# Pair features by products with neighbour steps spread over rows by DMA, a bf16 copy on ScalarE, and two shared PSUM banks

## The chip, the cores and the metric

The kernel runs on one core of a Trainium2 chip. The metric is the device time of one execution in microseconds. Three runs of the kernel before gave 366.8, 369.47 and 370.51 us; the median is 369.47 us. A separate, profiled execution is where all durations below come from.

In the profile, PE is TensorE (matrix products), PEld its weight loads, DVE is VectorE, ACT is ScalarE, POOL is GpSimd and SP is SyncE. POOL and SP here mostly issue DMAs. L505 means line 505 of the kernel before.

## The reference

An attention block with 32 inducing points is followed by a feed-forward layer. `x` has 4 batches of 12480 tokens with 128 channels; `inducing` has 32 rows.

```
def mab(q, kv):
    s = scale * (q @ kv.transpose(0, 2, 1))        # scale = 1 / sqrt(128)
    s = s - s.max(-1, keepdims=True)
    a = np.exp(s)
    a /= a.sum(-1, keepdims=True) + 1e-09
    return a @ kv
h = mab(I, x)              # 32 rows per batch, from all tokens
y = mab(x, h)              # every token, a mix of the 32 rows of h
u = y @ w_in               # 128 -> 2048
out = (u * np.clip(u + 3.0, 0.0, 6.0) / 6.0) @ w_out
```

## The kernel before

**The algebra.** A token's `y` is a weighted mean of the 32 rows `h_m`, so the output can be written as a linear part in the 32 normalised weights minus a part that is quadratic in them: for each pair of rows `(m, n)` a product of the two weights times a coefficient vector made from the square of `(h_m - h_n) @ w_in`. The 496 pairs are laid out as four blocks of 128 rows (the features). A feature is `exp(scale * (h_m + h_n) . x)`, the product of two unnormalised weights. So each token costs four features of 128 rows, one 128x128 matmul for each, one linear matmul, and one multiplication by the inverse of the squared sum of the weights.

**Tiling.** A batch has six groups of 2048 tokens and a last one of 192. A group has four chunks of 512 tokens (the last group one chunk of 192), so there are 25 chunks per batch, 100 in all. In a chunk the tokens are four slices of 128.

**Three kinds of work.**

- *Stage a* of a batch (`a_T`, `a_s1`, `a_agg`), per group: 16 transposes of a bf16 copy of x on TensorE into a PSUM tile `pt`, each half copied by DVE into `xT` (L214, L215); 16 score matmuls into `s1` (L222), one exp on ACT (L228), then 16 aggregation matmuls that accumulate `exp @ x` in the bank `hnd` (L236) and a DVE sum of the weights (L247). x comes in from memory through POOL's DMA queue (L116). For batch 0 the bf16 copy is made half by DVE and half by ACT (L204, L205); for the other batches x is read a second time by a DMA that converts it (L120).
- *Stage c* of a batch (`c_sum` to `c_tail`): the 32 rows of h, their transpose `HT`, differences `dH` and sums `W` (L327 to L341); G, L and BD, the linear part (L349 to L393); and `c_sq`, 16 times: a matmul of `w_in` with `dH` into `dpm` (L400), its square, on ACT (L411) or in batch 0 every fourth time on DVE (L408, L409), and two units later four matmuls that accumulate the coefficients in the bank `cp` (L420). `c_tail` copies them to `Cq` (L433).
- *Stage b*, per chunk: `b_base` three times, a matmul of `W[:, k]` with the chunk's `xT` into a bank `bp` (L505) and an exp on ACT (L512), which gives T0, D1 and D2; three products on DVE, T1 = T0 D1, T2 = T0 D2, T3 = T2 D1 (L519, L528, L529); the linear matmul (L537) and 16 feature matmuls (L553) into a bank `op`; and the eviction, which multiplies by `r_all` on DVE (L569) and after each group's last chunk is followed by an output DMA on SP's queue (L576). Per group there are also `b_e`, four matmuls of 32 columns into four strips of one bank and an exp, `b_f` and `b_r`, which make the weights' sums and inverses.

**What sets the order.** The order on each engine is the order in which the program is written (a manual schedule); each engine works through its own list in order and waits where an operand isn't ready. The loop runs over chunks `t`. In iteration t the matmuls of chunk t are issued, the features of chunk t + 2 are begun (`LEAD = 2`), and the products of chunk t + 1 are finished. The per-group work is put into iterations shortly before the group's first chunk (`ahead`). Between these pieces the function `bg` puts units of background work, four times an iteration: the stages a and c of the next batch, as a list of 66 units spread evenly over the 25 iterations of this batch. Stage a and c of batch 0 run before the loop and in its first four iterations (the prelude); the last batch has no background work.

**PSUM.** There are eight banks: three rotating ones for `bp`, `ep`, `sp`, `rp` and other small results, two for `op`, one for `pt` and `dpm`, one for `s1` and `cp`, and one that `hnd`, `gp`, `lp` and `lt` use one after another. In batch 0 `pt` and `dpm` take turns over the `op` banks too.

Of the kernel before, what the change touches and what calls it, by code (L numbers as in the profile page):

```python
# [9 lines left out]
FP32 = mybir.dt.float32  # L10
# [15 lines left out]
SL = 4  # L26
LEAD = 2


def shifted(t, off, k_step, i_step):  # L30

    a = t[:, 0, 0:1]
    return bass.AP(
        tensor=a.tensor, offset=a.offset + off, ap=[a.ap[0], [k_step, 2], [i_step, 4], [1, 32]]
    )


def shifted1(t, off, i_step):

    a = t[:, 0, 0:1]  # L40
    return bass.AP(tensor=a.tensor, offset=a.offset + off, ap=[a.ap[0], [i_step, 4], [1, 32]])
# [3 lines left out]
def kernel(  # L45
# [38 lines left out]
    with ExitStack() as es:  # L84
# [3 lines left out]
        xin = es.enter_context(tc.tile_pool(name="xin", bufs=4))  # L88
# [3 lines left out]
        dp = es.enter_context(tc.tile_pool(name="dp", bufs=3))  # L92
# [3 lines left out]
        sqp = es.enter_context(tc.tile_pool(name="sqp", bufs=3))  # L96
# [15 lines left out]
        def load_x(b, g):  # L112
# [5 lines left out]
            if b > 0:  # L118
                tb = xbin.tile([P, TG, C], BF16, name="xb")
                nc.gpsimd.dma_start(tb[:p, :n, :], src)  # L120
                xbs[(b, g)] = tb

        for g in range(4):
            load_x(0, g)
# [23 lines left out]
        sel = sel[:, :, :].rearrange("k q m -> k (q m)")  # L148

# [32 lines left out]
        def side_bank(b, shape, dtype, name):  # L182

            if b == 0:
                turn[0] += 1
                if turn[0] % 3:
                    return psO.tile(shape, dtype, name=name, tag="op")
# [11 lines left out]
        def a_cast(g):  # L199
            t0, p, n = groups[g]  # L200
            h = n // 2
            xb = xbin.tile([P, TG, C], BF16, name="xb")
            xbs[(0, g)] = xb
            nc.vector.tensor_copy(xb[:p, :h, :], xs[(0, g)][:p, :h, :].bitcast(FP32))  # L204
            nc.scalar.copy(xb[:p, h:n, :], xs[(0, g)][:p, h:n, :].bitcast(FP32))  # L205
# [11 lines left out]
        def a_s1(b, g):  # L217
            t0, p, n = groups[g]
            st = S[b]
            s1 = psS.tile([P, 512], FP32, name="s1", tag="s1")  # L220
# [10 lines left out]
        def a_agg(b, g, h, a1):  # L231
# [18 lines left out]
            else:  # L250
                ahead = 4 if b == 0 else 2
                if g + ahead < NGR:
                    load_x(b, g + ahead)
                if b == 0 and g + ahead == NGR - 1:
                    load_weights()

        def a_units(b):
# [3 lines left out]
            for g in range(NGR):  # L261
# [6 lines left out]
                us.append(lambda g=g: a_T(b, g, 0))  # L268
                if late:
                    us.append(late.pop(0))  # L270
                us.append(lambda g=g: a_T(b, g, 1))
# [8 lines left out]
        def a_first():  # L280

            a_cast(0)
# [571 lines left out]
```

## Time and profile before

| | |
|---|---|
| runs | 366.8, 369.47, 370.51 us (median 369.47) |
| the profiled execution: time | 371.26 us |
| its span | 369.4 us |
| mean granted TensorE clock | 0.978 |
| busy: PE, DVE, ACT, POOL | 330.9, 284.4, 238.7, 28.7 us |
| DMA | 63.52 MB in 12516 packets |

The span is cut by stage: x loads and stage a of batch 0 until about 35 us, the prelude until about 59 us, three batch periods of about 83.5 us that carry the next batch's stages a and c, a last batch of about 50 us, and some 9 us at the end in which the last store lands.

How to read the rows: a row of the timeline has the start and the length in us, the engine, the line, what is written from what is read, and the count; in brackets stands how long the engine was idle before it, and what released it. Matmuls are pipelined, so the length of one is more than what it holds the engine for; the distance from one start to the next tells that. A row of the chain of waits has start, length and the work that the end of the run depended on. A row of a group by line has the shapes, the count, then busy us and mean ns, then the idle time before and its releasers.

### The profile page before, as it was taken

The page shows a single profiled execution, that of the slowest core. Times are in us where ns is not written, and L with a number is a line of the kernel's source. Part 1 is how long each engine was busy: PE and PEld are TensorE (multiplying, and loading weights), DVE is VectorE, ACT ScalarE, POOL GpSimd, SP SyncE. Part 2 cuts the span into 40 slices and gives each one's busy share as a digit, 9 for nine tenths or more (in the row PEclk, how much of TensorE's full clock was granted, in tenths as well). Part 3 has the DMA queues.
Part 4 walks back from the last instruction along what each step waited for, and adds up shares of the span by engine and source line. Part 5 has one row for each costly group of instructions (what it writes and reads, how often), then busy time and mean ns, then how long its engine had stood idle before and what let it go on. Part 6 is the DMA issues. An engine that isn't in the chain of part 4 may idle for free.

```text
span 369.4 us, 9414 instructions
## 1 busy us (share of the span) xinstructions
PE 330.9 (90%) x3926; PEld 246.8 (67%) x3926; DVE 284.4 (77%) x688; ACT 238.7 (65%) x442; POOL 28.7 (8%) x57
## 2 busy tenths in 40 slices
PE   1848977999989998999989998999989999999980
PEld 1737555887767675878757775888757766767760
DVE  3746577989897767989897767988887768999990
ACT  2432465666677875566667875566667887888840
POOL 3022001111100001111100001120000000000000
PEclk9988899999999999999999999999999999999995
DMA  7699802999982204998982204997022203222241
GB/s 271 232 350 241 287 0 31 307 277 216 300 262 114 115 3 142 291 295 207 313 262 118 112 4 135 280 291 237 16 101 115 113 4 126 115 114 115 115 184 67
DMA packets 12516, 63.52 MB, mean 172 GB/s; under 512 B 1280, under 2 KB 3504, under 8 KB 6192
## 3 DMA queue, kind: packets, MB, share of 16 engines
q0 software_dynamic: 8704, 37.24, 38.0%
q1 hardware_dynamic: 3760, 25.58, 17.0%
q8 instruction: 33, 0.54, 0.6%
q14 instruction: 19, 0.16, 0.1%
HBM read 46.84 MB, written 25.56 MB: 196 GB/s over the span
## 4 chain that ended last, share of the span: by engine, by line
PE 74%; DVE 14%; DMA 4%; ACT 4%; issue 2%; POOL 0%; POOLq 0%; DVEq 0%
PE op L553 22%; PE bp L505 14%; PE hnd L236 6%; PE pt L214 6%; PE op L537 5%; DMA xr<-in_x_dram 4%; PE dpm L400 4%; PE cp L420 3%; DVE os L569 3%; PE s L222 3%; PE ep L455 2%; PE rp L490 2%; PE gp L349 2%; PE sp L469 2%; DVE T L529 2%
## 5 line engine op out<-in xcount | busy, mean ns | idle before, releaser
L512 ACT ACTIVATE x<-bp 128x512 bf16<-128x512 f32 x300 | 170.8, 586 | 68.8 <-PE bp L505 60.8
L553 PE MATMUL op<-Cq,T 128*128 128x128 bf16 (+1 forms) x1200 | 130.6, 219 | 0.4
L505 PE MATMUL bp<-xT,W 128*128 128x512 bf16 x300 | 112.0, 374 | 0.0
L553 PEld LDWEIGHTS <-T 128*128 128x128 bf16 (+1 forms) x1200 | 84.2, 98 | 13.0 <-DVE T L529 0.8
L553 PE MATMUL op<-Cq,x 128*128 128x128 bf16 (+1 forms) x400 | 89.8, 224 | 0.0
L569 DVE TENSOR_TENSOR os<-op,r_all 128x512 f32<-128x512 f32 (+1 forms) x100 | 68.5, 685 | 21.0 <-PE op L553 20.3
L553 PEld LDWEIGHTS <-x 128*128 128x128 bf16 (+1 forms) x400 | 38.7, 97 | 27.9 <-issue 21.4
L519 DVE TENSOR_TENSOR T<-x,x 128x512 bf16<-128x512 bf16 (+1 forms) x100 | 41.4, 414 | 14.1 <-ACT x L512 13.4
L537 PE MATMUL op<-BD,nf 128*128 128x512 f32 (+1 forms) x100 | 51.9, 519 | 0.0
L529 DVE TENSOR_TENSOR T<-T,x 128x512 bf16<-128x512 bf16 (+1 forms) x100 | 41.8, 418 | 3.4
L215 DVE COPY xT<-pt 128x1024 bf16<-128x1024 bf16 (+1 forms) x56 | 34.4, 616 | 11.8 <-PE pt L214 11.7
L236 PE MATMUL hnd<-xr,a 128*32 128x128 f32 (+1 forms) x400 | 40.6, 244 | 1.5 <-ACT a L228 1.4
L528 DVE TENSOR_TENSOR T<-x,x 128x512 bf16<-128x512 bf16 (+1 forms) x100 | 40.9, 409 | 0.0
L214 PE MATMUL pt<-ident_b,xb 128*128 128x128 bf16 (+1 forms) x400 | 33.6, 230 | 7.5 <-DVE xT L215 4.1
L411 ACT ACTIVATE sq<-dpm 128x512 bf16<-128x512 f32 x60 | 35.4, 595 | 6.7 <-PE dpm L400 6.6
L214 PEld LDWEIGHTS <-xb 128*128 128x128 bf16 (+1 forms) x400 | 27.0, 104 | 13.6 <-issue 6.5
L236 PEld LDWEIGHTS hnd<-xr,a 128*32 128x32 f32 (+1 forms) x400 | 29.2, 113 | 7.5 <-ACT a L228 2.2
L420 PEld LDWEIGHTS <-sq 128*128 128x128 bf16 x256 | 19.1, 97 | 18.6 <-issue 5.7
L505 PEld LDWEIGHTS <-W 128*128 128x128 bf16 x300 | 29.3, 98 | 0.9
L420 PE MATMUL cp<-w6n,sq 128*128 128x128 bf16 x256 | 24.6, 219 | 2.2 <-DVE sq L409 2.2
L400 PE MATMUL dpm<-dH,w_in_b 128*128 128x512 bf16 x64 | 24.1, 379 | 2.0 <-ACT sq L411 1.7
L120 POOL DMA_DIRECT2D xb<-in_x_dram x21 | 11.1, 530 | 190.4 <-PE pt L214 125.9
(94 smaller groups left out, 304.9 us busy)
## 6 DMA issues: line engine op xcount, KB each, us to landing
xr<-in_x_dram POOLq DMA_DIRECT2D x24, 1024.0 KB, 7.8
out_dram<-os SPq DMA_DIRECT2D x24, 1024.0 KB, 4.3
xb<-in_x_dram POOLq DMA_DIRECT2D x18, 512.0 KB, 6.5
w_in_r<-in_moe_w_in_dram POOLq DMA_DIRECT2D x1, 1024.0 KB, 6.7
w_out_r<-in_moe_w_out_dram POOLq DMA_DIRECT2D x1, 1024.0 KB, 9.6
xr<-in_x_dram POOLq DMA_DIRECT2D x4, 96.0 KB, 7.1
out_dram<-os SPq DMA_DIRECT2D x4, 96.0 KB, 2.3
xb<-in_x_dram POOLq DMA_DIRECT2D x3, 48.0 KB, 2.6
```

The lines of the kernel that those rows point to most:

```text
L214: nc.tensor.transpose(pt[:, (i - lo) * p : (i - lo + 1) * p], xb[:p, i, :], ident_b[:p, :p])
L236: nc.tensor.matmul(st["hnd"][:M, :C], lhsT=a1[:p, i * M : (i + 1) * M], rhs=xs[(b, g)][:p, i, :], start=(g == 0 and i == 0), stop=(g == NG ...
L400: nc.tensor.matmul(dpm[:, :], lhsT=w_in_b[:, jb * P : (jb + 1) * P], rhs=st["dH"][:, :, :, :, :].rearrange("p q k i m -> p (q k i m)"),)
L420: nc.tensor.matmul(st["cp"][:, k * C : (k + 1) * C], lhsT=sq[:, k * P : (k + 1) * P], rhs=w6n[:, jc, :], start=(jc == 0 and k == 0), stop= ...
L505: nc.tensor.matmul(bp[:, :w], lhsT=st["W"][:, k].rearrange("p i m -> p (i m)"), rhs=st["xT"][:, c0 : c0 + w],)
L512: nc.scalar.activation(t[:, :w], bp[:, :w], ACT.Exp, scale=scale)
L519: nc.vector.tensor_mul(T1[:, :w], st[("x", c, 0)][:, :w], st[("x", c, 1)][:, :w])
L528: nc.vector.tensor_mul(T2[:, :w], T0[:, :w], D2[:, :w])
L529: nc.vector.tensor_mul(T3[:, :w], T2[:, :w], D1[:, :w])
L537: nc.tensor.matmul(op[:p, :], lhsT=st[("nf", g)][:, j * p : (j + 1) * p], rhs=st["BD"][:, :], start=True, stop=False, skip_group_check=True,)
L553: nc.tensor.matmul(op[:p, s * C : (s + 1) * C], lhsT=T[k][:, s * p : (s + 1) * p], rhs=st["Cq"][:, k, :], start=False, stop=(s == SL - 1 a ...
L569: nc.vector.tensor_mul(ot[:p, j * SL : (j + 1) * SL, :], op[:p, :].rearrange("p (s c) -> p s c", c=C), r_all[:p, b, c, :].unsqueeze(2).to_ ...
```

## The change

Seven edits belong together.

1. **Features.** The pairs are laid out anew: T0 holds the pairs of rows at distance 2, 6, 10, 14, T3 those at distance 4, 8, 12, 16, with the four distances next to each other for one m. Both are made by a base matmul and an exp, so two per chunk in place of three. T1 and T2 (odd distances) are T0 times a factor that depends on m alone: `exp(scale * (h_{m+1} - h_m) . x)` and `exp(scale * (h_{m-1} - h_m) . x)`. So DVE makes two products per chunk in place of three.
2. **Pack and spread.** The two factors have 32 rows. `b_pack` makes them for a whole group at once: four matmuls of 32 columns, one for each chunk, into four strips of one bank, then one exp on ACT; twice per group. `b_spread` copies for each chunk and factor the 32 rows to 128, each row four times, by a DMA on SP's queue (128 KB written), four chunks ahead; the product that reads it is issued three iterations later.
3. **bf16 copy.** x is read once. ACT converts it from the fp32 tile in two halves per group, each put behind a burst of transposes (`a_cast`). Batch 0 keeps its split between DVE and ACT. x loads are issued four groups ahead in all batches, over the batch's end too.
4. **Banks.** `pt`, `s1` and `dpm` share two banks. `cp` moves to the bank that `hnd`, `gp`, `lp` and `lt` use.
5. **Squares.** The coefficient matmuls follow their square by six units instead of two, with eight buffers for squares instead of three; G, L and BD come earlier in the list of units. The list has 69 units.
6. **Tail.** The pairs at distance 16 count half. They are now every fourth row of the last block, so a column of factors `half_of`, made at the start, takes the place of a constant for a range of rows.
7. **Prelude.** The loop begins one iteration earlier, at t = -5.

```diff
@@ a_cast, in place of the second read of x
+        def a_cast(b, g, parts):
+            t0, p, n = groups[g]
+            if (b, g) not in xbs:
+                xbs[(b, g)] = xbin.tile([P, TG, C], BF16, name="xb")
+            xb = xbs[(b, g)]
+            for eng, lo, hi in parts:
+                lo, hi = lo * n // 4, hi * n // 4
+                eng(xb[:p, lo:hi, :], xs[(b, g)][:p, lo:hi, :].bitcast(FP32))
@@ a_units
+                def first(g=g):
+                    a_T(b, g, 0)
+                    if g + 1 < NGR:
+                        a_cast(b, g + 1, ((nc.scalar.copy, 0, 2),))
+                def second(g=g):
+                    a_T(b, g, 1)
+                    if g + 1 < NGR:
+                        a_cast(b, g + 1, ((nc.scalar.copy, 2, 4),))
@@ pools
-        dp = es.enter_context(tc.tile_pool(name="dp", bufs=3))
+        dpk = es.enter_context(tc.tile_pool(name="dpk", bufs=2))
+        dp = es.enter_context(tc.tile_pool(name="dp", bufs=4))
-        sqp = es.enter_context(tc.tile_pool(name="sqp", bufs=3))
+        sqp = es.enter_context(tc.tile_pool(name="sqp", bufs=8))
-        psX = es.enter_context(tc.tile_pool(name="psX", bufs=1, space=PSUM))
-        psS = es.enter_context(tc.tile_pool(name="psS", bufs=1, space=PSUM))
+        psX = es.enter_context(tc.tile_pool(name="psX", bufs=2, space=PSUM))
@@ c_HT
+            W = coef.tile([P, 2, M, 4], BF16, name="W")
+            nc.vector.tensor_add(W[:, :], shifted(HT, 0, 0, 0), shifted(HT, 2, 2, 4))
+            Wd = coef.tile([P, 2, M], BF16, name="Wd")
+            nc.vector.tensor_sub(Wd[:, 0], HT[:, :, :].rearrange("p a m -> p (a m)")[:, 1 : M + 1], HT[:, 0])
+            nc.vector.tensor_sub(Wd[:, 1], HT[:, :, :].rearrange("p a m -> p (a m)")[:, M - 1 : 2 * M - 1], HT[:, 0])
@@ c_sq
-            jc = jb - 2
+            jc = jb - CLAG
-                st["cp"] = psS.tile([P, 512], FP32, name="cp", tag="s1")
+                st["cp"] = psH.tile([P, 512], FP32, name="cp", tag="hnd")
@@ c_units
+            us = [lambda: c_sum(b)] + gap + [lambda: c_den(b)] + gap + [lambda: c_HT(b)] + gap
+            us += sq[0:1] + [lambda: c_G(b, 0), lambda: c_G(b, 1)] + sq[1:3]
+            us += [lambda: c_L(b, 0), lambda: c_L(b, 1)] + sq[3:5] + [lambda: c_BD(b)]
+            us += sq[5:] + [lambda: c_tail(b)]
@@ new
+        def b_pack(b, g, k):
+            t0, p, n = groups[g]
+            st = S[b]
+            J = n // SL
+            w = SL * p
+            pp = psF.tile([P, 512], FP32, name="pp", tag="fb")
+            for j in range(J):
+                nc.tensor.matmul(
+                    pp[32 * j : 32 * j + 32, :w],
+                    lhsT=st["Wd"][:, k],
+                    rhs=st["xT"][:, t0 + j * w : t0 + (j + 1) * w],
+                    tile_position=(0, 32 * j),
+                )
+            t = dpk.tile([P, 512], BF16, name=f"dk{k}")
+            nc.scalar.activation(t[: 32 * J, :w], pp[: 32 * J, :w], ACT.Exp, scale=scale)
+            st[("dk", g, k)] = t
+        def b_spread(b, c):
+            g, j = chunks[c]
+            st = S[b]
+            w = SL * groups[g][1]
+            for k in range(2):
+                d = dp.tile([P, 512], BF16, name=f"d{k}")
+                nc.sync.dma_start(
+                    d[:, :w],
+                    st[("dk", g, k)][32 * j : 32 * j + 32, :w].unsqueeze(1).to_broadcast([32, 4, w]),
+                )
+                st[("d", c, k)] = d
+        def b_prod(b, c):
+            st = S[b]
+            w = SL * groups[chunks[c][0]][1]
+            T0, T3 = (st.pop(("x", c, k)) for k in range(2))
+            T = [T0]
+            for k in range(2):
+                d = st.pop(("d", c, k))
+                t = tp.tile([P, 512], BF16, name=f"T{1 + k}")
+                nc.vector.tensor_mul(t[:, :w], T0[:, :w], d[:, :w])
+                T.append(t)
+            st[("T", c)] = T + [T3]
@@ the loop
+                ahead.setdefault(t - LEAD - 3, []).append(lambda b=b, g=g: (b_pack(b, g, 0), b_pack(b, g, 1)))
...
+        for b in range(1, B):
+            for i, h in enumerate((0, 2)):
+                ahead.setdefault((b - 1) * NCK + i - 2, []).append(
+                    lambda b=b, h=h: a_cast(b, 0, ((nc.scalar.copy, h, h + 2),))
+                )
...
-        for t in range(-LEAD - 2, total):
+        for t in range(-LEAD - 3, total):
...
+            if 0 <= t + 4 < total:
+                b_spread(*divmod(t + 4, NCK))
             if 0 <= tb - 1 < total:
-                b_T23(*divmod(tb - 1, NCK))
+                b_prod(*divmod(tb - 1, NCK))
...
-            if feat:
-                b_base(fb_, fc, 1)
             bg(0.5)
-            if feat:
-                b_T1(fb_, fc)
...
             if feat:
-                b_base(fb_, fc, 2)
+                b_base(fb_, fc, 1)
```

More of the change, by code (lines that the diff above doesn't have):

```diff
@@ L26 @@
 SL = 4
+XBUF = 4
+CLAG = 6
 LEAD = 2
@@ L117, in load_x @@
             xs[(b, g)] = t
[L118 to L123, printed above, removed]
+        for g in range(XBUF):
             load_x(0, g)
@@ L280, in a_first @@
         def a_first():
-            a_cast(0)
+            both = ((nc.vector.tensor_copy, 0, 2), (nc.scalar.copy, 2, 4))
+            a_cast(0, 0, both)
             late = None
@@ L621 @@
         done_units = [0]
[L622 to L624 removed]
+        n_units, span = len(queue), (LEAD + 3)
+        begin = -LEAD - 3
+        for t in range(-LEAD - 3, total):
             if t >= 0 and t % NCK == 0:
@@ L630 @@
                 if b + 1 < B:
-                    for g in range(2):
-                        load_x(b + 1, g)
                     a_begin(b + 1)
```

84 lines of the change are left out of this document (30 added, 54 removed).

## The prediction

> **What bounds the kernel now.** I read the head of the page, then the busy time by stage, then single stretches of the timeline to find the pace of each kind of matmul, and last the chain of waits. All times below are of the profiled execution, which took 371.26 us (span 369.4 us and 1.9 us around it), 1.8 us over the median of 369.47 us.
>
> ```profile
> span 369.4 us, 9414 instructions
> PE 330.9 (90%) x3926; PEld 246.8 (67%) x3926; DVE 284.4 (77%) x688; ACT 238.7 (65%) x442; POOL 28.7 (8%) x57
> ```
>
> By stage (columns: busy us and count of PE, weight load, DVE, ACT, POOL; then the granted clock and the DMA share):
>
> ```profile
> 143.00:190.00 47.00, 45.49 (x617) 35.66 (x617) 39.99 (x90) 29.92 (x54) 7.46 (x14) 1.00 0.93 251
> 190.00:223.50 33.50, 31.99 (x336) 22.88 (x333) 24.77 (x67) 26.10 (x53) 0.00 (x0) 1.00 0.24 98
> 223.50:307.00 83.50, 80.24 (x978) 60.34 (x977) 67.27 (x161) 58.02 (x109) 4.75 (x9) 1.00 0.45 143
> ...
> 324.58:332.91 8.33, 8.33 (x93) 5.88 (x90) 7.83 (x20) 7.22 (x14) 0.00 (x0) 1.00 0.30 126
> ...
> 46.00:58.90 12.90, 9.88 (x99) 6.69 (x96) 9.61 (x21) 8.18 (x18) 0.00 (x0) 1.00 0.00 1
> ```
>
> The first two rows are the two halves of a batch period that carries background work: stage a (transposes, scores and aggregation of the next batch) and stage c (its coefficients). The third row is a whole such period, 83.5 us; there are three. The fourth is one group of four chunks in the last batch, with no background; the fifth the prelude before the first output. TensorE is busy throughout at full clock, so the question is whether it works or waits. The pace of each matmul is the distance from its start to the next one's:
>
> ```profile
> 326.53 0.40 PE L455 MATMUL ep<-xT,HTb 128*32 128x512 bf16 x4
> ...
> 326.86 0.23 PE L553 MATMUL op<-Cq,x 128*128 128x128 bf16 x1
> ...
> 327.09 0.38 PE L505 MATMUL bp<-xT,W 128*128 128x512 bf16 x1
> ...
> 327.31 0.22 PE L553 MATMUL op<-Cq,x 128*128 128x128 bf16 x1
> ...
> 327.37 0.33 PE L553 MATMUL op<-Cq,T 128*128 128x128 bf16 x3
> ...
> 327.53 0.38 PE L505 MATMUL bp<-xT,W 128*128 128x512 bf16 x1
> ```
>
> A base matmul (L505) holds TensorE 327.31 - 327.09 = 0.22 us, four feature matmuls (L553) 0.22 us, four strip matmuls of 32 columns (L455) together 0.33 us. The last batch runs without gaps at this pace: TensorE is its bound (DVE 7.83 and ACT 7.22 of 8.33 us). For the background work the chain gives the pace:
>
> ```profile
> 146.75 0.45 PE pt L214 x8
> 148.45 0.48 PE hnd L236 x8
> ...
> 158.39 0.50 PE s L222 x16
> ...
> 43.65 0.22 PE cp L420 x4
> 43.87 0.22 PE dpm L400
> 44.31 0.85 PE gp L349 x8
> ...
> 49.39 0.48 PE lp L373 x8
> ```
>
> One batch of it is 12.5 x 0.45 + 12.5 x 0.48 + 6.25 x 0.50 + 16 x 0.22 + 16 x 0.22 + 2 x 0.85 + 2 x 0.48, about 24.4 us, with some 0.7 for the small ones 25. Twenty-five chunks are 6 x 8.33 + about 1.5 for the short one, 51.5. Of 83.5 us that leaves 7 us in which TensorE waits, more than its idle time shows.
>
> **The change part by part.**
>
> *Features.* Per group of four chunks, four base matmuls go (4 x 0.22 = 0.88 us) and two packs of four strip matmuls come. No pack is in the trace; L455 has the same shape (32 columns, 512 moving, four strips), so I take 2 x 0.33 = 0.66. Bounds: 0.44 if the pair costs what two single base matmuls do, 1.76 if the strips run one after another. Saving 0.22 per group, over 24 groups 5.3 us, all on the bound. That strip matmuls cost 0.11 us over one full matmul is in the rows. The Trainium skill, TensorEngine Tiling (Array Packing), Key Properties, says that a change of tiling mode drains TensorE; by that rule two packs in a row would pay once, 0.55, and the saving would be 7.9 us.
>
> ```profile
> L512 ACT ACTIVATE x<-bp 128x512 bf16<-128x512 f32 x288 | 167.3, 597 | 68.5 <-PE bp L505 60.6 <-DVE os L569 1.2 <-DVE T L528 0.6
> L528 DVE TENSOR_TENSOR T<-x,x 128x512 bf16<-128x512 bf16 x96 | 39.9, 416 | 0.0
> L205 ACT CAST xb<-xr 128x1024 bf16<-128x1024 f32 x6 | 6.2, 1041 | 10.1 <-DMA xr<-in_x_dram 10.1
> L576 SPq DMA_DIRECT2D out_dram<-os x28: 331/332/359, 74.0 to 360.5; - x28
> ```
>
> DVE loses one product of 0.42 per chunk; ACT loses one exp of 0.60 per chunk and gains two per group; at 83.5 / 25 = 3.34 us per chunk the stretch of stage a is 14.1 chunks long. In the last batch DVE falls to 7.83 - 1.67 = 6.2 and ACT to 7.22 - 2.39 + 1.19 = 6.0 of 8.1: TensorE stays the bound.
>
> *The bf16 copy.* Stage a gets 12 casts of 1.04: ACT there 29.9 - 14.1 x 0.60 + 7.1 x 0.60 + 12.5 = 38.2 of 47 us (81%); DVE 40.0 - 5.9 = 34.1 (73%). ACT runs in order, so behind each cast stand base and pack exps, and TensorE waits for them when its three feature banks are full. A base matmul needs the bank of three allocations earlier, over a microsecond of TensorE work, so a single cast is mostly covered and a cast on top of a backlog is not. Bounds 0 and 1.04 per cast; I take 0.8 us per batch. In the other direction, 21 second reads of x leave the queue of POOL, with no one waiting for them: nothing.
>
> *Two shared banks.* At a batch's start the second burst of transposes waits for the one bank, whose copy stands behind an eviction and two products on DVE:
>
> ```profile
> 224.95 0.61 PE L214 MATMUL pt<-ident_b,xb 128*128 128x128 bf16 x8
> ...
> 225.63 0.68 DVE L569 TENSOR_TENSOR os<-op,r_all 48x512 f32<-48x512 f32 x1
> ...
> 226.24 0.41 DVE L528 TENSOR_TENSOR T<-x,x 128x512 bf16<-128x512 bf16 x1
> ...
> 227.02 0.69 DVE L215 COPY xT<-pt 128x1024 bf16<-128x1024 bf16 x1
> 227.76 0.61 PE L214 MATMUL pt<-ident_b,xb 128*128 128x128 bf16 x8 [1.47 <-DVE xT L215]
> ...
> 294.87 0.38 PE L505 MATMUL bp<-xT,W 128*128 128x512 bf16 x1
> ...
> 295.54 0.38 PE L400 MATMUL dpm<-dH,w_in_b 128*128 128x512 bf16 x1 [0.29 <-ACT sq L411]
> ```
>
> That is 1.47 us per batch; a dpm matmul waits for the square of the one before (295.54 - 294.87 - 0.22 = 0.45 here). With two banks I take off 1.5 + 1.0 = 2.5 of the 7 us; bounds 0 and 7. What is late next: cp now lives in the bank of hnd, gp, lp and lt. Its first matmul must wait for the four copies of lt to BD, and L follows G after two units of squares instead of three, while three DVE operations read gp:
>
> ```profile
> 51.98 0.27 ACT BD L393
> ...
> 52.88 0.31 DVE BD L393
> ...
> 53.20 0.70 DVE d L408
> ...
> 54.67 0.40 PE cp L420 x4
> ...
> 55.98 0.70 DVE d L408
> ...
> 57.52 0.41 PE cp L420 x4
> ```
>
> The four BD copies take 53.19 - 51.98 = 1.2 us. I add 0.9 us per batch for both waits (bounds 0 and 3.3: the 1.2 and three DVE steps of an eviction's 0.7, uncovered).
>
> *Sum for a batch with background:* -6 x 0.22 - 2.5 + 0.8 + 0.9 = -2.1; three of them -6.3, the last batch -1.3.
>
> *Prelude.* In this chain cp waits twice for a square made on DVE (53.20 to 54.67 and 55.98 to 57.52, 3.0 us). With a lag of six matmuls and eight buffers both leave the chain. Against that: two packs on TensorE and 3.3 us more on ACT (two casts 2.1, four pack exps 2.4, less two base exps 1.2), which was busy 8.18 of 12.9 us. I take -2.0; bounds -3.0 and +1.5. The one-column operations at the start and the rearranged H differences replace work of like size or lie ahead of DMA waits: 0.
>
> *Spread.* Per chunk SP issues two more DMAs, 2 x 0.33 us, behind the output store's wait for the eviction. A product needs them three chunks later, 6 us in the last batch. A DMA's cost I take from:
>
> ```profile
> q1 hardware_dynamic: 3760, 25.58, 17.0%
> out_dram<-os SPq DMA_DIRECT2D x24, 1024.0 KB, 4.3
> out_dram<-os SPq DMA_DIRECT2D x4, 96.0 KB, 2.3
> ```
>
> A 128 KB spread lands in about 2.4 us by the last two rows, behind a store in about 5: hidden. 0.17 x 369.4 / 25.58 = 2.45 us of all engines per MB by the first, so 0.31 per spread by bytes. The trace has no packets like its 128 of 1 KB each; if small packets cost three times their bytes, 0.93. I take the lower end.
>
> *Total:* 371.3 - 6.3 - 1.3 - 2.0 = 361.7; at the level of the median, less 1.8, **360 us** (-2.6%).
>
> **Rivals.**
>
> *ACT holds TensorE (slower).* Every cast lands on a backlog, and half of it (0.52) reaches TensorE through the three feature banks in stage a: 36 x 0.52 = 18.7 in place of my 2.4, so 378 - 1.8 = 376. It decides where ACT stands more than about 1.4 us behind TensorE. For: 81% in stage a, in order, with pack exps in pairs. Against: 29.9 of 47 now leaves room, and DVE, whose copies free the other banks, gets lighter. 0.10.
>
> *Spreads late.* Above 0.089 us per 1-KB packet a pair takes over 1.42 us and, with 0.61 of store per chunk, exceeds the 2.03 us of a chunk in the last batch. At three times the bytes: 2 x 0.93 + 0.61 = 2.47, 25 x 0.44 = 11 us more, 371. Against: two x streams leave, and by bytes the share is a third of that. 0.07. The Trainium skill, DMA: Bandwidth & Descriptors, Issuing engines are not separate DMA queues, says that transfers from all issuers interleave on the same 16 engines; the trace agrees, with a DMA share of 0.93 in stage a where loads and stores meet.
>
> *The waits only change place.* Bank waits return in the shared coefficient bank and at ACT, the prelude keeps its length: 371.3 - 5.3 - 1.8 = 364. For: the 7 us have many causes. 0.15.
>
> *All cover holds.* No new waits, half the 7 us gone, prelude -3.0: -3 x (1.3 + 3.5) - 1.3 - 3.0 = -18.7, 351. For: DVE and ACT both stay under 82%. 0.20.
>
> *Strips don't overlap,* so the change doesn't halve anything: 24 x 1.1 = 26 more, 386. Against: 0.33 us for four. 0.03.
>
> **How the numbers follow.** The forecast has 0.45, with its own range of 356 to 365. About 1% (365.8 to 373.2) is what a measurement can tell from no change. Faster: 0.43 + 0.20 + half of 0.15, 0.70; same: the rest of these and most of the late spreads, 0.15; slower 0.15. Leaving out ACT, strips and most of the late spreads, and reaching to 351 and past 364 to the uncertain costs, the range is 350 to 369.
>
> **What would show it.** Right: a last-batch group of 8.1 us with TensorE still without gaps; two packs 0.6 to 0.7 us apart from the next matmul; no 1.47-us wait at batch starts; the first output matmul about 2 us sooner; periods near 81.4 us. Wrong: base matmuls waiting for ACT in stage a, or products waiting for DMA.

## The result and the profile after

The changed kernel took 355.91 us (median of 4 runs, 354.64 to 362.76), the kernel before 369.19 us in runs beside it: ratio 0.9636, 95% interval 0.956 to 0.9711. Forecast were 360 us and a range of 350 to 369. The profiled execution of the changed kernel took 354.64 us. First its page: span, busy time by engine, the two DMA queues (packets, MB, share of 16 engines), and the group of products that read spread tiles (busy us and mean ns, then idle time before and its releaser).

```profile
span 352.8 us, 10094 instructions
...
PE 321.2 (91%) x4001; PEld 238.6 (68%) x4026; DVE 245.5 (70%) x592; ACT 239.3 (68%) x440; POOL 17.6 (5%) x37
...
q1 hardware_dynamic: 32560, 51.15, 47.8%
q0 software_dynamic: 5920, 27.66, 25.2%
...
L569 DVE TENSOR_TENSOR T<-T,d 128x512 bf16<-128x512 bf16 (+1 forms) x200 | 74.1, 409 | 7.2 <-DMA d<-dk 6.9
```

DVE lost 39 us of busy time, ACT as good as nothing, and TensorE, the bound, 10 us. The time by stage says more. Columns as in the prediction: busy us of PE, weight load, DVE, ACT, POOL, then the granted clock and the DMA share. Rows one, two and five are the three periods, from the first output matmul of one batch to that of the next; three and four are stages a and c of the second; the last is a group of the last batch.

```profile
54.01:136.63 82.62, 78.55 (x1000) 58.70 (x1004) 57.42 (x136) 60.96 (x113) 3.74 (x7) 1.00 0.73 227
136.63:216.56 79.93, 78.13 (x1000) 58.71 (x1004) 57.49 (x136) 60.97 (x113) 3.73 (x7) 1.00 0.76 242
136.63:182.00 45.37, 44.45 (x620) 34.20 (x621) 35.25 (x79) 35.06 (x60) 3.73 (x7) 1.00 0.84 267
182.00:216.56 34.56, 33.68 (x382) 24.52 (x385) 22.24 (x58) 25.90 (x53) 0.00 (x0) 1.00 0.66 209
216.56:295.84 79.28, 77.47 (x992) 58.21 (x996) 56.83 (x135) 59.41 (x112) 1.57 (x3) 1.00 0.65 188
300.30:308.40 8.10, 8.10 (x95) 5.60 (x95) 6.15 (x16) 5.85 (x12) 0.00 (x0) 1.00 0.76 229
```

The same code runs in all three periods, but the first is 2.7 us longer than the second; 2.3 of it lie in two chunks (13 and 14: 9.05 us against 6.76). The third lacks 0.6 us in its last chunk, as in every kernel here. The table has the periods of every profiled execution, read at the first output matmul of each batch (us from the span's start; "last" is from the first output matmul of the last batch to the first of its last chunk). Each ratio is to runs of the kernel before on the same chip.

| kernel | median us | ratio to before (95%) | first output | periods 0, 1, 2 | last |
|---|---|---|---|---|---|
| before | 369.19 | 1 | 58.6 | 83.2, 83.6, 82.9 | 48.6 |
| after | 355.91 | 0.9636 (0.956 to 0.9711) | 54.0 | 82.6, 79.9, 79.3 | 46.3 |
| after, again | 357.36 | 0.9669 (0.9638 to 0.97) | 56.6 | 81.2, 81.0, 79.3 | 46.3 |
| features alone | 383.33 | 1.0404 (1.0349 to 1.0459) | 54.9 | 89.2, 89.1, 88.8 | 46.3 |
| all but features | 360.19 | 0.9795 (0.9763 to 0.9827) | 54.3 | 82.0, 81.3, 80.7 | 48.4 |
| old banks, lag, order | 368.21 | 1.0015 (0.9966 to 1.0064) | 55.2 | 85.1, 85.3, 81.6 | 46.3 |
| bf16 copy by a second read | 488.23 | - | 53.9 | 131.6, 126.2, 105.5 | 46.3 |
| the same, issued first | 386.41 | 1.0541 (1.0485 to 1.0596) | 55.1 | 87.0, 92.6, 85.5 | 46.3 |
| transposes and scores apart | 369.33 | 0.9846 (0.9794 to 0.9898) | 55.6 | 82.8, 82.3, 81.6 | 46.3 |
| no casts | 361.13 | - | 54.8 | 85.7, 88.9, 79.2 | 46.3 |
| spreads one chunk earlier | 353.69 | 0.9623 (0.9588 to 0.9658) | 57.3 | 79.7, 79.2, 78.5 | 46.6 |
| the same, later start | 352.74 | 0.958 (0.9559 to 0.9601) | 54.2 | 79.7, 79.2, 78.5 | 46.6 |
| strips together | 356.76 | 0.9684 (0.964 to 0.9728) | 54.4 | 81.9, 81.7, 79.8 | 45.5 |

Some executions of these kernels ran longer, most of them at a lower mean granted clock, among them seven of ten of "transposes and scores apart" (one at 1698.59 us) and three of four of "no casts" (the second try); the medians hold them, the ratios leave them out (no ratio where one execution alone is left), and these two kernels are judged by periods.

Between the two profiled executions lie 16.6 us: 4.6 before the first output, 0.6 + 3.6 + 3.7 in the periods, 2.3 in the last batch, 1.8 behind it. Some 4 of the first 4.6 seem to belong to that one execution of the kernel before: its bf16 copy of the transposed seeds, the end of stage a of batch 0, began 40.8 us into the span, and 35.8 to 38.1 us in eleven others (the first try of "no casts" left aside), one of which (features alone, 36.8) has the old code for this stage. In that execution TensorE stood idle for 4.0 us from 20.6 us on (1.8 at most in the others), and ahead of the copy the granted clock was 0.50 twice, from 25.7 and from 36.0 us, for 3.4 us each.

Of the 1.8 us at the end, 1.0 is the last store, which landed after 3.0 and 2.0 us; of the "some 9 us in which the last store lands" it is the smaller part. From the last feature matmul to the end of the span it takes 11.1 to 11.5 us in the four profiled kernels that read x twice and 8.8 to 9.9 in the ten that read it once. Why was not traced.

### The profile page after: what moved, and what is told of

Same layout as the page of the kernel before. It is cut to its first block, busy times and chain, and to the rows that moved or that the text cites. A ratio compares the mean times of both kernels' runs of the same rounds, so it can differ in the third digit from the quotient of the medians.

```text
span 352.8 us, 10094 instructions
## 1 busy us (share of the span) xinstructions
PE 321.2 (91%) x4001; PEld 238.6 (68%) x4026; DVE 245.5 (70%) x592; ACT 239.3 (68%) x440; POOL 17.6 (5%) x37
## 5 line engine op out<-in xcount | busy, mean ns | idle before, releaser
L594 PE MATMUL op<-Cq,T 128*128 128x128 bf16 (+1 forms) x1600 | 147.5, 220 | 0.5
L558 ACT ACTIVATE T<-bp 128x512 bf16<-128x512 f32 (+1 forms) x200 | 112.4, 593 | 42.6 <-PE bp L552 30.6
L594 PEld LDWEIGHTS <-T 128*128 128x128 bf16 (+1 forms) x1600 | 98.0, 98 | 42.4 <-issue 26.4
L569 DVE TENSOR_TENSOR T<-T,d 128x512 bf16<-128x512 bf16 (+1 forms) x200 | 74.1, 409 | 7.2 <-DMA d<-dk 6.9
L552 PE MATMUL bp<-xT,W 128*128 128x512 bf16 (+1 forms) x186 | 69.4, 374 | 0.8 <-DVE d_all L328 0.8
L206 ACT CAST xb<-xr 128x1024 bf16<-128x1024 f32 (+1 forms) x49 | 46.8, 963 | 9.6 <-DMA xr<-in_x_dram 9.6
L216 DVE COPY xT<-pt 128x1024 bf16<-128x1024 bf16 (+1 forms) x56 | 34.4, 618 | 11.8 <-PE pt L215 11.5
L529 ACT ACTIVATE dk<-pp 128x512 bf16<-128x512 f32 (+1 forms) x56 | 28.2, 554 | 13.3 <-PE pp L522 12.7
L215 PEld LDWEIGHTS <-xb 128*128 128x128 bf16 (+1 forms) x400 | 25.7, 101 | 10.5 <-DVE xb L206 4.2
L111 POOL DMA_DIRECT2D xr<-in_x_dram x28 | 15.1, 539 | 219.2 <-ACT xb L206 127.9
L229 ACT ACTIVATE a<-s 128x512 fp32r<-128x512 f32 (+1 forms) x28 | 15.5, 553 | 15.0 <-PE s L223 15.0
L436 PEld LDWEIGHTS <-sq 128*128 128x128 bf16 x256 | 18.6, 98 | 9.2 <-DVE BD L409 1.4
L487 DVE CUSTOM_DVE_ANT_0 nf<-e,sp 128x512 fp32r<-128x512 f32 (+1 forms) x28 | 17.2, 613 | 4.7 <-PE sp L485 4.2
```

The lines of the kernel that those rows point to most:

```text
L206: eng(xb[:p, lo:hi, :], xs[(b, g)][:p, lo:hi, :].bitcast(FP32))
L215: nc.tensor.transpose(pt[:, (i - lo) * p : (i - lo + 1) * p], xb[:p, i, :], ident_b[:p, :p])
L216: nc.vector.tensor_copy(st["xT"][:, t0 + lo * p : t0 + hi * p], pt[:, : (hi - lo) * p])
L436: nc.tensor.matmul(st["cp"][:, k * C : (k + 1) * C], lhsT=sq[:, k * P : (k + 1) * P], rhs=w6n[:, jc, :], start=(jc == 0 and k == 0), stop= ...
L552: nc.tensor.matmul(bp[:, :w], lhsT=st["W"][:, k].rearrange("p m i -> p (m i)"), rhs=st["xT"][:, c0 : c0 + w],)
L558: nc.scalar.activation(t[:, :w], bp[:, :w], ACT.Exp, scale=scale)
```

## The experiments

**1. The parts one by one.** The first kernel takes the one before and gives it the new features, packs, spreads and products only; the second takes everything else and leaves the features. Both start the loop one iteration earlier.

```diff
# features alone, against before: only this
-  W[:, 0], W[:, 1], W[:, 2]; b_base x3; b_T1, b_T23
+  W, Wd; b_pack, b_spread, b_base x2, b_prod; half_of
# all but features, against before: only this
+  a_cast on ACT, x read once; psX bufs=2; cp in psH; CLAG = 6; new c_units
```

> The kernel before with the new features alone (two bases, packs, spreads, two products); x is read twice, the banks, the lag and the order of the units are those of before. Theory 'parts add up' (TensorE work 5.3 us less, the waits of before stay): 369.2 - 5.3 = 364, and batch periods of about 82 us. Rival 'DVE relief' (a product less per chunk on DVE removes most of the waits by itself, the banks were not the cause): 369.2 - 10 or more, 359 or less, periods near 80 us.

> The kernel before with everything but the new features: casts on ACT, two shared banks, cp in the coefficient bank, lag of six, new order of units; three bases, three exps and three products per chunk stay. Theory 'parts add up': the banks and the lag take off about 7, the casts add up to 2.4: 364 to 365. Rival 'ACT is the limit' (29.9 + 12.5 = 42.4 of 47 us busy in stage a): no gain or slower, 369 to 374, with base matmuls waiting for ACT in stage a.

Measured: 383.33 and 360.19 us. The features that were to save 5.3 us cost some 15 when they come alone (383.33 against 367.59 of the kernel before on that chip), though the last batch, which loads no x, has the same gain as in the full change (48.6 to 46.3). So the loss lies where x is loaded. In each of the three periods chunk 8 took 8.8 to 9.1 us (3.6 in the changed kernel). The DMA view of features alone around that chunk (155 to 178 us):

```profile
q0 software_dynamic: 998, 4.90, 72.8%
q1 hardware_dynamic: 1818, 2.64, 34.4%
...
d<-dk SPq DMA_DIRECT2D x9, 128.0 KB, 13.0
```

Its waits there (engine, line, what was waited for: us in total, times, longest):

```profile
DVE T L573 <- DMA d<-dk: 6.7, 4, 3.9
```

The DMA view of the changed kernel, at the same place of a period (148 to 171 us):

```profile
q1 hardware_dynamic: 1775, 3.42, 41.3%
q0 software_dynamic: 427, 2.68, 40.7%
...
d<-dk SPq DMA_DIRECT2D x14, 128.0 KB, 8.1
```

With x read twice the load queue alone takes 73% of the 16 engines, the two queues together all of them, and a spread lands after 13.0 us; with x read once it takes 41%, and a spread lands after 8.1 us, within the three chunks until its product (some 10 us). The single read doesn't merely leave a queue: it makes room for the spreads.

The wait is not all of the 5.5 us that chunk 8 loses. Features alone around it (171.8 to 180.9 us; columns as above, the granted clock third from the end):

```profile
171.00:174.60 3.60, 1.49 (x17) 0.99 (x14) 0.38 (x2) 1.37 (x3) 1.11 (x2) 1.00 1.10 305
174.60:181.40 6.80, 6.05 (x54) 4.37 (x54) 5.05 (x12) 2.39 (x4) 0.00 (x0) 0.50 1.04 364
```

While the products wait, TensorE is busy 1.5 of 3.6 us, and then the granted clock is 0.50 for 6.8 us. At half pace that is up to 3.4 us of its work, an estimate from this row. The late spreads of experiments 2, 4 and 5 are followed by such stretches too.

**2. Banks, lag and order put back.**

```diff
-  psX bufs=2 (pt, s1, dpm); cp in psH; CLAG = 6; sqp bufs=8; G, L, BD early
+  psX bufs=1 (pt, dpm), psS bufs=1 (s1, cp); CLAG = 2; sqp bufs=3; old list of units
```

> The changed kernel with the banks, the lag of two and the order of units of before; features and casts stay. Theory 'parts add up': about 7 of the 13 us come back, 362 to 363, with the 1.5-us wait of the transposes at batch starts. Rival 'DVE relief': 356 to 358, the waits are gone without the second bank.

Measured: 368.21 us, all the gain gone. Two things stand in its periods: 81.6 in the quiet period 2 against 79.3, which is the banks, and some 3 us more in periods 0 and 1 each, at chunks 13 to 16, where products again wait for spreads and the granted clock is 0.50 for 3.4 us in either period. This kernel and features alone differ by the reads of x alone (casts, or a second read, and when x is loaded): with the old banks the second read costs 383.33 - 368.21 = 15 us.

**3. Which of the three.** Only the banks are parted again; `cp`, the lag of 6 and the new order stay.

```diff
-  psX bufs=2 (pt, s1, dpm)
+  psX bufs=1 (pt, dpm), psS bufs=1 (s1)
```

> The changed kernel with the two shared PSUM banks parted again, one for the transposes and one for the scores, while the coefficients stay in the third bank, the lag of 6 and the new order of units stay. Putting back banks, lag and order together cost 12.3 us, of which 2.3 us a period in periods without late spreads. Theory A, it is the banks: 362 to 368 us, and the transposes wait for the copy of the bank before. Theory B, it is the lag and the order of units: 355 to 358 us. Theory C, half each: 359 to 361 us.

Measured: ratio 0.9846, its three shortest executions 362.1 to 363.6 us. Period 2 of three kernels: transposes and scores apart; everything put back (experiment 2); all but features.

```profile
220.68:302.32 81.64, 78.28 (x990) 58.28 (x996) 56.87 (x135) 59.98 (x112) 1.58 (x3) 1.00 0.63 183
```

```profile
225.61:307.18 81.57, 78.39 (x998) 58.37 (x996) 56.44 (x135) 60.06 (x112) 1.57 (x3) 1.00 0.62 183
```

```profile
217.69:298.41 80.72, 79.35 (x973) 59.80 (x971) 66.99 (x160) 65.04 (x122) 1.57 (x3) 1.00 0.28 105
```

81.64 against 79.28 is 2.36 us a period for the second shared bank; lag, order and the place of `cp` together add 81.57 - 81.64, nothing, as long as the banks are parted; beside shared banks they were not tried. Theory A held, at its lower end. By chunks, 0.8 lie in the first, where the transposes wait for DVE's copy again (0.7 us), and 1.7 in chunks 16 to 21, among the coefficients' matmuls. The 80.72 gives the features 1.44 us a period (80.72 - 79.28).

**4. The second read itself.** The changed kernel with the bf16 copy by DMA instead of by casts.

```diff
-  a_cast(b, g + 1, ...)                       # on ACT, both halves
+  load_xb(b, g + 2), behind load_x(b, g + 4) in POOL's queue
```

> The changed kernel with the bf16 copy made by a second read of x as before, no casts on ACT after batch 0. Theory 'casts cost 0.8 per batch': 355.9 - 2.4 = 353.5, and the first batch period as long as the others if the casts are why it is longer. Rival 'casts are covered': 356 within 1. Rival 'DMA is short': slower, 358 or more, since another megabyte per group delays the spreads, with more idle time of DVE for them than the 6.9 us of the changed kernel.

Measured: 488.23 us, a third more than before. Around the worst place (POOL's issues with the idle time before them, then TensorE's transposes):

```profile
94.67 0.52 POOL L111 DMA_DIRECT2D xr<-in_x_dram  x1 [16.58 <-PE op L599]
95.18 0.58 POOL L118 DMA_DIRECT2D xb<-in_x_dram  x1
...
101.50 1.04 PE L222 MATMUL pt<-ident_b,xb 128*128 128x128 bf16 x8 [5.10 <-DMA xb<-in_x_dram]
```

The load of xr stands first in POOL's queue and needs the tile that the aggregation matmuls (up to 94.4 us) have just let go. The load of xb behind it had its tile long before, but POOL issues in order, so it left only then, and TensorE stood from 96.4 to 101.5 us until it landed. That is a circle between a queue and an engine, made by my edit, and says nothing of bandwidth. Over its three periods the granted clock is 0.84, with fourteen stretches at 0.50, so up to 58 of the 121 us that they are longer are the slower clock behind such stands (an estimate: 0.16 x 363 us). To break the circle, the same once more, with the load of xb put ahead, right behind the transposes that free its tile:

```diff
                 def second(g=g):
                     a_T(b, g, 1)
+                    if g + 2 < NGR:
+                        load_xb(b, g + 2)
```

> The changed kernel with the bf16 copy of x again loaded by a second read from batch 1 on, but issued ahead of the next full-precision load in GpSimd's queue, so that it never waits behind a load that has no free slot. No casts on ScalarE after batch 0. Theory A, the DMA engines cannot carry the second read and the spreads together in the transpose stage: as where the features were put alone into the kernel before, one chunk of each period takes some 5 to 6 us longer since its spread lands late; three periods, less the 0.8 us of casts in each, give 355.9 + 15 = 371 us (364 to 378). Theory B, only the order in GpSimd's queue made the earlier form slow, and a second read is as free as it was before: 355.9 - 3 x 0.8 = 353.5 us (351 to 356).

Measured: 386.41 us: theory A, and more of it than expected. Its spreads at 155 to 178 us, then two waits over the whole span:

```profile
d<-dk SPq DMA_DIRECT2D x11, 128.0 KB, 13.0
```

```profile
DVE T L574 <- DMA d<-dk: 25.8, 13, 4.3
...
PE pt L222 <- DMA xb<-in_x_dram: 1.7, 4, 0.7
```

Everything else is as in the changed kernel, which took 357.36 us on this chip, so a second read in place of the casts costs 386.4 - 357.4 = 29 us here. TensorE waits only 1.7 us for the read itself; the products wait 25.8 for spreads (6.9 in the changed kernel), and the granted clock is 0.50 for 17 us of the three periods: most of the loss comes by way of late spreads. Leaving out the casts alone brings late spreads as well (experiment 5), so the share of the read itself is not parted from theirs.

**5. No casts.** The transposes of batches 1 to 3 read one stale tile of batch 0, so these batches' scores and features are made from other data, and the casts are left out.

```diff
-  a_cast(b, g + 1, ((nc.scalar.copy, 0, 2),)) and its second half, for b > 0
+  xbs[(b, g)] = xbs[(0, NGR - 2)]
```

> The changed kernel without any bf16 copy of x after batch 0: the transposes of batches 1 to 3 read one stale tile of batch 0, so those outputs are those of other data; this leaves out 21 casts in two halves each on ScalarE and the waits on them. It prices the casts. Theory A, as predicted, they cost 0.8 us a batch: 355.9 - 2.4 = 353.5 us (352.5 to 354.5). Theory B, they are hidden, as ScalarE is 76% busy in the transpose stage: 355 to 356.5 us. Theory C, ScalarE in its program order is what holds the transpose stage: 350 us or less.

> The changed kernel without the bf16 copy of x after batch 0 (stale data in the transposes of batches 1 to 3), once more, since the granted clock was 0.56 in the profiled execution of the first try and 0.96 in the others. Theory A, as predicted, casts cost 0.8 us a batch: 2.4 us less than the changed kernel beside it. Theory B, they are hidden: within 1 us of it. Theory C, they hold the transpose stage: 5 us less or more.

Measured: no price in the totals. The first try gave 364.37 us (ratio 0.9816, 0.9758 to 0.9874), and its profiled execution took 514.89 us at a granted clock of 0.56; the second gave 361.13 us (355.19 to 368.45). Period 2 of the second try has no late spread and full clock:

```profile
219.40:298.60 79.20, 77.96 (x998) 58.44 (x996) 57.09 (x133) 49.47 (x98) 1.58 (x3) 1.00 0.65 190
```

ACT has 10 us less to do there, and the period is 0.1 us shorter (79.28 to 79.20): the casts are hidden. Periods 0 and 1 were 3 and 9 us longer than in the changed kernel, almost all at chunks 13 to 16, the place of the late spreads, and there the granted clock is 0.50 for 6.8 and 13.7 us: up to 3.4 and 6.8 us of TensorE's work. Period 1:

```profile
183.00:188.30 5.30, 1.96 (x21) 1.24 (x20) 2.85 (x6) 1.11 (x3) 0.00 (x0) 1.00 1.04 391
188.30:202.00 13.70, 13.61 (x72) 9.64 (x71) 8.10 (x21) 4.93 (x11) 0.00 (x0) 0.50 0.33 99
```

A wait of a few us thus became a period longer by 9. Whether the casts, by holding tiles of x longer, keep the loads from meeting the spreads there, was not tried.

**6. Late spreads.** In period 0 of the changed kernel, 94 to 108 us, a store, a load and eight spreads met. Its DMA issues (KB each, median us to landing):

```profile
out_dram<-os SPq DMA_DIRECT2D x1, 1024.0 KB, 10.4
d<-dk SPq DMA_DIRECT2D x8, 128.0 KB, 8.5
xr<-in_x_dram POOLq DMA_DIRECT2D x1, 1024.0 KB, 10.0
```

Its waits there:

```profile
DVE T L569 <- DMA d<-dk: 4.2, 3, 1.9
```

So the spreads and packs were put one chunk earlier, first with the loop's start one iteration earlier too, then with the start left alone:

```diff
-        dp = es.enter_context(tc.tile_pool(name="dp", bufs=4))
+        dp = es.enter_context(tc.tile_pool(name="dp", bufs=5))
-                ahead.setdefault(t - LEAD - 3, []).append(... b_pack ...)
+                ahead.setdefault(max(t - LEAD - 4, -LEAD - 3), []).append(... b_pack ...)
-            if 0 <= t + 4 < total:
-                b_spread(*divmod(t + 4, NCK))
+            if t == -4:
+                b_spread(0, 0)
+            if 1 <= t + 5 < total:
+                b_spread(*divmod(t + 5, NCK))
```

> The changed kernel with the spreads and packs issued one chunk (about 3.2 us) earlier and five instead of four buffers for each kind of spread tile. In the changed kernel period 0 is 3.3 us longer than period 2, at its chunks 0, 1, 13 and 14, where VectorE waited 1.28, 0.97 and 1.92 us for spreads. Theory A, these spreads start too late: all these waits are shorter than a chunk, so they go, 355.9 - 3.3 - 0.6 = 352 us (350.5 to 353.5). Theory B, the DMA engines are full there, and an earlier start only moves the queue, or the earlier pack finds ScalarE and the PSUM ring busier: 355 to 357 us.

> The changed kernel itself, so that the two below stand beside it on one chip. 353 to 358 us; period 0 longer than period 2 by about 3 us again, if its late spreads belong to the kernel; within 1 us of it, if they were an accident of the profiled execution.

> The changed kernel with spreads and packs one chunk earlier, but with the first group of batch 0 left where it was, so that the loop starts no earlier. The form before it had periods of 79.7, 79.2 and 78.5 us (the changed kernel: 82.6, 79.9, 79.3) and gave part of it back: 1.5 us more between the transposed seeds and the first output, 0.3 us in the last batch. Theory A, the periods keep their gain and the start costs nothing: 4.5 us less than the changed kernel beside it, less 0.3: 351 to 352 us, ratio to it 0.988. Theory B, the start of the loop has to wait for the same chain anyway, or the late spreads of period 0 were an accident: 1 us or less between the two.

Measured: 353.69 us; 357.36; and 352.74 us, whose interval (0.9559 to 0.9601) lies below that of the changed kernel on the same chip (0.9638 to 0.97). The periods of the last one:

```profile
54.20:133.90 79.70, 79.09 (x1007) 59.24 (x1004) 57.43 (x136) 61.57 (x115) 3.75 (x7) 1.00 0.74 233
133.90:213.00 79.10, 78.74 (x1005) 59.14 (x1003) 57.17 (x136) 60.51 (x113) 3.75 (x7) 1.00 0.78 244
213.00:291.50 78.50, 78.14 (x998) 58.69 (x996) 56.70 (x135) 58.75 (x111) 1.58 (x3) 1.00 0.64 189
```

TensorE is busy 99% of each, no product waits for a spread any more, and six runs lie between 350.8 and 353.4 us where six of the changed kernel lay between 355.2 and 372.5. Some 0.8 us a period is gained even against a period without late spreads (79.93 to 79.15), by the other place of the packs or otherwise; that was not taken apart. In "after, again" the late spreads fell elsewhere: 0.9 us in chunk 16 of period 0, 1.1 in chunks 12 to 16 of period 1. So they belong to the kernel, and where they fall changes from one execution to the next. The two forms reach the first output at 57.3 and 54.2 us in their profiled executions, while their medians are 1 us apart. The first has two more stretches of 3.4 us at a granted clock of 0.50 ahead of it (from 32.8 and 43.0 us), which is up to 3.4 us of TensorE's work, so what the extra iteration cost is open. The version with the later start beats both kernels.

**7. What a strip costs.** The chain of waits of the changed kernel in the last batch (start, length, work):

```profile
302.30 0.46 PE op L594 x8
302.76 0.55 PE pp L522 x8
303.31 0.33 PE op L594 x4
303.64 0.22 PE bp L552
303.85 0.22 PE op L594 x4
...
304.52 0.46 PE op L594 x8
304.98 0.33 PE ep L471 x4
305.31 0.33 PE op L594 x4
305.64 0.22 PE bp L552
```

Eight strip matmuls take 0.55 us, four 0.33: 0.055 each and 0.11 once. Behind either, four full matmuls (a quad) take 0.33 in place of 0.22, another 0.11. The chain of the kernel before has the same behind its own strips:

```profile
326.60 0.33 PE ep L455 x4
326.93 0.33 PE op L553 x4
327.26 0.22 PE bp L505
```

The chain goes from end to end. Measured from start to start, as the prediction did it, the extra 0.11 lies ahead of the strips; a visit costs 0.22 more than its strips either way. If that is the price of changing between full and strip matmuls, then packs and `ep` side by side pay it once instead of twice:

```diff
-                ahead.setdefault(max(t - LEAD - 4, -LEAD - 3), []).append(... b_pack(b, g, 0), b_pack(b, g, 1))
-                ahead.setdefault(t - LEAD - 2, []).append(... b_e(b, g))
-                ahead.setdefault(t - LEAD - 1, []).append(... b_f(b, g))
+                s = {0: -5, 4: -2}.get(t, t - LEAD - 5)
+                ahead.setdefault(s, []).append(... b_pack(b, g, 0), b_pack(b, g, 1), b_e(b, g))
+                ahead.setdefault(t - LEAD - 2, []).append(... b_f(b, g))
```

> The kernel with spreads one chunk earlier (352.74 us) with the strip matmuls of a group put side by side: the two packs and the four strip matmuls of the group's own exponentials (ep) follow one another, two chunks earlier than the latter stood; the step after them (sp) one chunk earlier. In the profiles each visit of the strips costs 0.11 us on the way in (four strips 0.33, eight 0.55) and 0.11 on the way out (the four full matmuls behind it take 0.33 in place of 0.22). Theory A, TensorE pays for each change between full and strip matmuls, whatever number of strips stands between: one visit a group instead of two, 0.22 us over some 23 groups, 5.1 us less, 347.7 us (346 to 350), and in the last batch twelve strips take 0.77 with one slow quad behind them. Theory B, three exponentials in a row on ScalarE and three PSUM buffers for all of them hold the base matmul behind, and the gain is lost in waits of the bases and quads: 352 us or more.

Measured: 356.76 us, slower than the 352.74 it started from. Its chain of waits in the last batch:

```profile
300.69 0.55 PE pp L522 x8
301.23 0.22 PE ep L471 x4
301.45 0.33 PE op L594 x4
301.78 0.32 PE bp L552
```

The mechanism of theory A is there: `ep` falls to 0.22 us, one slow quad is left, and the last batch is 1.1 us shorter (46.6 to 45.5). In the periods theory B wins. Period 2, where a group's packs follow those of the short last group:

```profile
279.06 1.34 ACT L529 ACTIVATE dk<-pp 128x512 bf16<-128x512 f32 x2 [0.62 <-DMA d<-dk]
...
279.71 0.38 PE L552 MATMUL bp<-xT,W 128*128 128x512 bf16 x1 [0.49 <-ACT dk L529]
```

The pack's exp on ACT waits for the spreads that still read its tile, and the base matmul waits for that exp to give up one of three PSUM buffers. That is 0.5 us of the 1.2 that this period loses; the rest, and the 2.3 and 2.6 us of the other two, were not traced.

## Why the prediction was right, point by point

The median is 4 us below the forecast of 360, just under the forecast's own range (356 to 365). Several steps were off and partly cancel, so that the forecast came this close is in part luck: the quiet periods gained 1.6 us each more than forecast, the last batch 1.0, and the end 1.8 that the sum did not have; against them the prelude gave none of its 2.0, and the late spreads made period 0 some 3 us longer. One of the prediction's own signs of being wrong, products waiting for DMA, did show (6.9 us in all).

- **TensorE's pace, its being the bound.** Right: a last-batch group at 8.10 us with no gap (forecast 8.1), DVE 6.15 (6.2) and ACT 5.85 (6.0).
- **Packs.** -0.22 us a group, measured 8.33 - 8.10 = 0.23; over a period 1.44 (forecast 1.3). The 0.66 for two packs came out by luck, from two errors that cancel. The row of 0.33 for four strips was doubled to 0.66; the pair takes 0.55. The Trainium skill, TensorEngine Tiling (Array Packing), Key Properties, says that a change of tiling mode drains TensorE; the trace agrees, with 0.11 us for eight strips as for four. But a second 0.11 for the change on the other side was left out of the sum; with it the packs cost 0.66 after all, and the saving of 7.9 us did not follow. It stood in the trace of before (the slow quad at 326.93 in the chain of experiment 7); from start to start it lies ahead of 326.53, where the quoted rows begin.
- **Banks.** Taken 2.5, measured 2.36 us a period.
- **Casts.** Taken +0.8 a batch, measured +0.1. ACT stands at 35.06 of 45.37 us in stage a, 77% (forecast 81%), and the cover holds. The rival in which ACT holds TensorE falls by the same row.
- **New waits at the shared bank, L close behind G.** Taken +0.9, measured nothing net in a period (lag, order and the place of `cp`, 81.57 against 81.64, with the banks parted).
- **A quiet period** thus changed by -1.44 - 2.36 + 0.1 = -3.7 us, which is what it did (82.94 to 79.28); the forecast was -2.1. The step that failed is the two costs on the other side, +1.7 in all.
- **Last batch.** -1.3 forecast, -2.3 measured: 1.2 in the groups, and 1.1 in the first chunk and the last four, which I had counted at the pace of the others. What made these faster was not traced.
- **Prelude.** -2.0 forecast; from the copy of the seeds to the first output it took 17.8 before and 18.2 us after, and 18.1 to 18.6 in the first three experiments. The 18.2 holds 3.4 us at a granted clock of 0.50 (from 38.8 us); the kernels of experiment 4 in its first form and of experiment 5, with the same prelude and no such stretch there, took 17.65. So 0.2 us at most was gained, with or without the features, with either lag. I had counted two waits of `cp` for squares as removable; what became late in their place I can't show by a run.
- **The second reads of x "leave, with no one waiting for them: nothing".** Wrong, and the largest error, though it hardly touched the sum: beside the spreads the second reads in place of casts cost 15 us with the old banks and 29 with the new. Whoever takes this change apart finds a loss in one half of it.
- **Spreads.** By bytes I took 0.31 us of all engines for each. By the two rows of queue q1, 0.478 x 352.8 - 0.170 x 369.4 = 105.8 us for 200 spreads, 0.53 each. That is under the 0.93 at which I had bounded it and under the rival's threshold (0.53 x 16 / 128 = 0.066 us a packet, against 0.089), so in the last batch nothing waited long (0.7 us at most). But a spread was to land in 2.4 us, or 5 behind a store, and took 3.9 (median) and 8.1 to 8.5 beside loads and stores; its issue on SP took 0.60 us (median) where 0.33 was taken. "Hidden" was wrong elsewhere: where a store and a load meet them in a period, products wait, and two chunks of period 0 were 2.3 us longer for it in the profiled execution. The rival of late spreads had its price in the wrong place.
- **"All cover holds" (351)** was nearest for the quiet periods: its -1.3 - 3.5 = -4.8 against the -3.7 measured. With the late spreads removed the kernel came to 352.74.

## What to carry to other kernels

A stream that nobody waits for can still set the time, if it uses the engines that a short, urgent transfer needs: before adding small transfers with a lead of a few microseconds, add up what all queues move in the stretch where they run, and give the lead by the landing time under that load, not by the landing time in quiet. A wait that leaves TensorE idle can cost more than itself: look at the granted clock behind it. Parts of a change need not add: here one alone cost 4%, the rest gained 2%, and together they gained 3.6%. Compare a stage over its repetitions in one trace, since the difference between equal periods shows waits that are only sometimes there.

## What the runs showed of the hardware

- Changing between full matmuls and strips of 32 columns cost 0.11 us on the way in and 0.11 on the way back, however many strips stood between (4, 8 and 12 were seen).
- Behind stretches in which late spreads or loads left TensorE idle for much of the time, the granted clock was 0.50 for 3.4 us or a multiple (3.4 to 13.7): features alone, 6.8 us behind 3.6 us that were 41% busy; no casts, 13.7 behind 5.3 that were 37% busy. In the changed kernel 8 us around 100 us that were 67% busy were followed by none, and with spreads one chunk earlier and the later start there was none between the first output and the last.
- A 128 KB spread in packets of 1 KB landed in 3.9 us (median of 192), 8.5 where a store and a load ran beside it, and 13.0 where x was read twice; its packets took 0.066 us each on average, against 2.45 us of all engines per MB for the store, which is 0.31 us for 128 KB.
- A load that waits for its tile at the head of POOL's queue held another that was ready: 488 us, and 386 in the other order.
